# A small fetch of q ahead of lam, fillers regrouped, and three pieces of work moved between engines, in a linear-attention kernel with an MLP

## The chip, the cores and the metric

The kernel runs on one core of a Trainium2 chip. The metric is the device time of one execution in microseconds (us), given as the median of several runs. A profile is one more execution of the same program, recorded by the hardware. The core has five engines that run side by side, each through its own list of instructions in order: PE (TensorE, matmuls and transposes), DVE (VectorE), ACT (ScalarE), POOL (GpSimd) and SP (SyncE, here only for starting DMAs). DMAs are started from SP, ACT or POOL; one that is started from ACT or POOL stands in that engine's list like any other instruction.

## The reference

The first half is causal linear attention with a decay `lam` per head, over B = 4 batches, H = 8 heads, S = 768 positions, D = 64 features; the second is an MLP over the 3072 tokens that come out of it, 512 to 2048 to 512 features.

```python
for b in range(nb):                                  # blocks of positions
    intra = einsum('bhic,bhjc->bhij', qb, kb) * Dmask        # lam ** (i - j) for i >= j, else 0
    intra = einsum('bhij,bhjd->bhid', intra, vb)
    inter = einsum('bhid,bhde->bhie', qb * lam_pow, kv_state)
    out[:, :, sl] = intra + inter
    kv_state = lam_block * kv_state + einsum('bhsd,bhse->bhde', kb * rev_pow, vb)
x = out.transpose(0, 2, 1, 3).reshape(B * S, H * D)
h = x @ w_in
result = (h / (1 + exp(-1.702 * h))) @ w_out
```

## The kernel before, in words

**Tiling.** The positions are cut into windows of 128 (`NW` = 6). The first two windows, w = 0 and w = 1 (`w < ND`), are special: each holds 256 positions of two batches, worked as two halves c = 0 and c = 1 (one batch each), with pairs of neighbouring positions folded into one row. The four later windows hold 128 positions of all four batches. Each window gives 512 tokens, and each goes through the MLP as soon as its attention is done.

**What a half of a window goes through.** `load_one` (L84) fetches k, q and v. For c = 0 of window 0, k and q and v come in two DMAs each, heads 0 to 3 and heads 4 to 7 ("groups" g = 0 and g = 1). `do_cast` (L202) multiplies k or q by powers of lam and turns it to bf16; an argument says on which engine, and g picks one group. `turn_pe` (L239) transposes the result on PE with an identity, and a copy (L219 on DVE or L222 on ACT) brings it from PSUM to SBUF as `kT` or `qT`. `cast_v` (L216 on POOL, L222 on ACT) turns v to bf16, in two copies for the first two windows. `d_scores` (L260) multiplies kT by qT, `d_masks` (L271) masks the scores into `sm`, `d_out` (L320) multiplies by v, `d_one` and `d_state` (L283) form the state, `d_inter` (L302) adds its part, and `d_x` copies the sum into `xT`, the input of the MLP.

**Powers of lam.** `lam` is fetched as one row (L105, a DMA started from ACT), spread over 128 partitions by a small fp32 matmul (`lam_p`, L151), and turned on ACT into ln(lam) (L153) and into powers (`kd_pow` and `qd_pow`, L156). ACT loads a function table ahead of that (L110) and another one behind it (L663). The first cast, of k, reads `kd_pow`.

**Fillers.** `fill(n)` (L147) issues n matmuls over a tile of zeros; no one reads their result. They stand in PE's list between the real work of the first 10 us.

**The order.** Everything behind L656 is in an order written out by hand: each engine executes its own instructions in the order of the program, and an instruction waits for the data it reads. For the opening this is: powers; cast and transpose k and then q of half c = 0; POOL waits for q's second group (`gate_pool`, L651, a copy of one element), then starts the DMA of the first piece of `w_in` and of v of c = 1; scores and masks of c = 0; then half c = 1, whose k is cast by POOL (g = 0) and by DVE (g = 1); then `w_in`'s other four pieces and `w_out` are fetched from POOL's list. `end(0, 1)` finishes window 0.

**The MLP.** Window 0 multiplies by `w_in` directly (`mlp1_half` L418, `mlp1` L406, one block `fc` of 128 features at a time) and for `w_out` uses a scheme with seven products in place of eight (`product`, L468), which needs sums of the halves of the weights (`weight_sums`, L432) and of the activations (`g_sums`, L445), formed by DVE. Later windows do the same for `w_in` (`in_product`, L559), with sums of its blocks that `in_sums(g)` forms once (L535) for each of four groups g of blocks. The steps of a window are a string: "I1" is `in_sums(1)`, "gl3" is one `g_sums`, "W01234" is one `weight_sums`, "u" is the end of one product. `GROUPS` (L515) names the blocks of each group: group 0 is blocks 4, 13, 14, 15; group 2 is blocks 5 to 8. Group 0 is the first that window 1's products use. `w_in` lies in five tiles of 2, 3, 4, 4 and 3 blocks; where the blocks of a pair lie in different tiles, as in group 0, `in_sums` issues eight subtractions in place of four.

**Window 1.** Its loads are started by SP behind a gate (L654) that waits for a piece of `w_out`. Its half c = 1 has k and q cast by POOL and both copies of v by ACT; `end(1, 0)`, `scores(1, 1)` and `end(1, 1)` finish its halves, with window 0's last products and window 1's first blocks of the MLP between them.

Of the kernel before, what the change touches and what calls it, by code (L numbers as in the profile page):

```python
# [25 lines left out]
def kernel(  # L26
# [13 lines left out]
    nc = tc.nc  # L40
    f32 = mybir.dt.float32
    bf16 = mybir.dt.bfloat16
    B, H, S, D = q.shape
    P = 128
# [20 lines left out]
    const = ctx.enter_context(tc.tile_pool(name="const", bufs=1))  # L65
# [36 lines left out]
                    load_one(w, c, nm, src[nm])  # L102

    lam_r = const.tile([1, H], f32)
    nc.scalar.dma_start(out=lam_r, in_=bass.AP(tensor=lam.tensor, offset=lam.offset, ap=[[0, 1], [1, H]]))  # L105
    ones = const.tile([1, P], f32)
    nc.vector.memset(ones, 1.0)
# [35 lines left out]
    def fill(n, new=None):  # L143
        if new:
            fill_ps[0] = acc("ps_fill", shape=[P, W], tag=new)
        for _ in range(n):
            nc.tensor.matmul(fill_ps[0], zero[:, 0:P], zero, start=True, stop=True)  # L147

    fill(4, "mm")
    lam_p = ps.tile([P, H], f32, tag="a", bufs=5, name="lam_p")  # L150
    nc.tensor.matmul(lam_p, ones, lam_r, start=True, stop=True)  # L151
    ln_lam = const.tile([P, H], f32)
# [40 lines left out]
    def do_cast(w, c, nm, eng, g=None):  # L193
        if g in (None, 0):
            cast[w, c, nm] = work.tile([P, NP, 2, P] if w < ND else [P, 2, HD], bf16, tag=f"{nm}s{c}",
                                       bufs={"k": 2, "q": 1}[nm], name=f"{nm}s")
        f, x = loaded[w, c, nm], cast[w, c, nm]
        if w < ND:
            pw = {"k": kd_pow, "q": qd_pow}[nm]
            for R in (0, 1) if g is None else (g,):  # L200
                h = slice(4 * R, 4 * R + 4)
                eng.tensor_tensor(x[:, 2 * R : 2 * R + 2].rearrange("p i a (j d) -> p j (i a) d", j=2),  # L202
                                  f[:, h].rearrange("p (j i) (a d) -> p j (i a) d", j=2, a=2),
                                  pw[:, h].rearrange("p (j i) a -> p j (i a)", j=2).unsqueeze(3).to_broadcast([P, 2, 4, D]),
                                  op=MUL)
        else:
            pw = {"k": k_pow, "q": q_pow}[nm]
            n = 2 * H // 4
            for j in range(2):
                eng.tensor_tensor(x.rearrange("p b (r i j d) -> p j (b r) i d", i=2, j=2, d=D)[:, j],  # L210
                                  f.rearrange("p h (a d) -> p (h a) d", a=2).rearrange("p (n j i) d -> p j n i d", j=2, i=2)[:, j],
                                  pw.rearrange("p b (r j i) -> p j (b r) i", i=2, j=2)[:, j].unsqueeze(3).to_broadcast([P, n, 2, D]),
                                  op=MUL)
# [436 lines left out]
    def gate_pool(x):  # L650
        nc.gpsimd.tensor_copy(behind_q, x)  # L651
# [4 lines left out]
    with tc.manual_schedule():  # L656
        for x, i in ((k_pow, i_k), (q_pow, i_q)):
            nc.scalar.activation(x, ln_lam.unsqueeze(1).to_broadcast([P, 2, H]), EXP, scale=i)
        mk_pow(inv_pow, -1.0 * P)
        for j, rows in enumerate((A, Z)):  # L660
            nc.scalar.activation(blk_pow[rows].rearrange("p (r i) -> p r i", i=2),
                                 ln_lam[rows].rearrange("p (r j i) -> p r j i", i=2, j=2)[:, :, j, :], EXP, scale=1.0 * P)
        nc.scalar.activation(warm, q_pow[:, 0, 0:1], GELU)  # L663
        fill(3)
        for nm, copies in (("k", (dve_copy, act_copy)), ("q", (act_copy, dve_copy))):
            for g in range(2):
                do_cast(0, 0, nm, nc.vector, g)
            for g in range(2):
                turn_pe(0, 0, nm, copies[g], g)
                fill(2 - g if nm == "k" else 1 - g)  # L670
        gate_pool(loaded[0, 0, "q"][0:1, H // 2, 0:1])
        load_w_in(0)
        load_one(0, 1, "v", v)
        cast_v(0, 0, (act_copy, act_copy))
        for pp in range(2):
            d_scores(0, 0, pp)
            d_masks(0, 0, pp)
        fill(3)
        do_cast(0, 1, "k", nc.gpsimd, 0)
        for j in range(1, len(IN_CH)):  # L680
            load_w_in(j)
        d_one(0, 0, "mm")
        d_keep(0, 0)
        turn_pe(0, 1, "k", act_copy, 0)
        oa, oz = d_out(0, 0, ("mm", "mm"))
        nc.scalar.copy(seen, oz[:, 3, P - 1 : P])
        do_cast(0, 1, "q", nc.vector, 0)
        do_cast(0, 1, "k", nc.vector, 1)
        do_cast(0, 1, "q", nc.vector, 1)
        turn_pe(0, 1, "q", act_copy, 0)  # L690
        d_inter(0, 0, oz, 0, False)
        turn_pe(0, 1, "k", act_copy, 1)
        d_state(0, 0, states[0, 0], Z)
        turn_pe(0, 1, "q", dve_copy, 1)
        d_x(0, 0, 0, oa, act_copy)
        d_x(0, 0, 1, oz, act_copy)
        cast_v(0, 1, (act_copy, pool_copy))
        for j in range(NCH):
            load_w_out(j)
        for pp in range(2):  # L700
            d_scores(0, 1, pp)
            d_masks(0, 1, pp)
        nc.gpsimd.affine_select(mask, mask, pattern=[[0, 1], [1, P]], channel_multiplier=-1, base=0,
                                compare_op=mybir.AluOpType.is_ge, fill=0.0)
        gate_sync(w_out_sb[1][0:1, 0, 0:2])
        load(1)
        mlp1_half(0, 0, 0)
        d_one(0, 1)
        d_keep(0, 1)
        act_copy(kv_sb[0][:, 0], states[0, 0])  # L710

        def scores(w, c):
            for pp in range(2):
                d_scores(w, c, pp)
            for pp in range(2):
                d_masks(w, c, pp)

        def end(w, c):
            oa, oz = d_out(w, c)
            t = acc("ps_kv", shape=[P, NP, D]) if w else states[w, c]  # L720
            if w == 0:
                nc.scalar.copy(seen, oz[:, 3, P - 1 : P])
            d_state(w, c, t, Z)
            if w == 0:
                d_inter(w, c, oz, 0, False)
            if w and c == 0:
                d_one(w, 1)
            d_x(w, c, 0, oa, act_copy)
            d_x(w, c, 1, oz, act_copy if w and c else dve_copy)
            if w:  # L730
                nc.vector.tensor_tensor(kv_sb[0][:, 2 * w + c], kept[w, c], t, op=ADD)
            else:
                nc.scalar.copy(kv_sb[0][:, 2 * w + c], t)
            if w and c == 0:
                d_keep(w, 1)

        def steps(w, names):
            for s in names.split():
                one_step(w, s)

        end(0, 1)
        for c, fc in ((0, 2), (1, 0), (1, 2)):
            mlp1_half(0, c, fc)
        for fc in range(4, FFC):
            mlp1(0, fc)
            steps(0, {5: "I1", 7: "I3", 9: "I0 gl3 gl1", 11: "W01234 gl2", 13: "W11234 gl4"}.get(fc, ""))
        steps(0, "p1a gh3 gh1 p2a W23124 p1b p2b gh2 gh4 p7l p4l W33124 p1h p2h p7h")
        do_cast(1, 0, "k", nc.vector)
        do_cast(1, 0, "q", nc.vector)
        steps(0, "p6l")  # L750
        turn_pe(1, 0, "k", act_copy)
        steps(0, "p6h")
        turn_pe(1, 0, "q", act_copy)
        steps(0, "p4h o")
        load(2, "kq")
        cast_v(1, 0, (pool_copy, act_copy))
        do_cast(1, 1, "k", nc.gpsimd)
        steps(0, "P50")
        scores(1, 0)
        d_one(1, 0)  # L760
        d_keep(1, 0)
        steps(0, "P51")
        d_even(1, 0, "mm")
        turn_pe(1, 1, "k", act_copy)
        cast_v(1, 1, (act_copy, act_copy))
        do_cast(1, 1, "q", nc.gpsimd)
        steps(0, "P30")
        end(1, 0)
        steps(0, "u I2")
        turn_pe(1, 1, "q", act_copy)  # L770
        steps(0, "P31")
        halves = [(c, fc) for c in range(HF) for fc in HALVES]
        for i, (c, fc) in enumerate(halves):
            if i == 1:
                scores(1, 1)
                d_even(1, 1)
            if i == 3:
                end(1, 1)
            if i == 4:
                x_sums(1)  # L780
            mlp1_half(1, c, fc)
            if i in (1, 2, 3, 4):
                nm = "kq"[(i - 1) % 2]
                do_cast(2, (i - 1) // 2, nm, nc.gpsimd)
                turn_dma(2, (i - 1) // 2, nm)
            if i == 6:
                load(2, "v")
        steps(1, STEPS[1])
        for w in range(ND, NW):
            steps(w, STEPS[w])  # L790
# [30 lines left out]
```

## Time and profile before

| | |
|---|---|
| median of 3 runs | 191.92 us (191.89 to 194.59) |
| the profiled execution's own time | 192.3 us |
| its span, first to last instruction | 190.6 us |
| PE busy | 184.3 us, 2296 matmuls |
| DVE busy | 152.0 us |
| ACT busy | 129.8 us |
| POOL busy | 50.7 us |

A row of the timeline gives the start and the duration in us, the engine, the line of the kernel, the operation, what is written and read, and in brackets how long the engine stood idle ahead of it and what ended that. "PEld" is the load of weights into PE, which may overlap its matmuls; "ACTq", "SPq" and "POOLq" are the issuing sequencers of those engines. The chain of work that ended last is followed back from the last instruction of the program: at each step it goes to what released the instruction, or to the one before it on its engine, so what stands in the chain set the end. The profiled execution is one execution; durations are taken from it, and a difference worked out from them is set against the median of the runs.

### The profile page before, as it was taken

How to read it: one execution, taken by the hardware profiler on the slowest of the kernel's cores; microseconds unless marked ns; L12 is line 12 of the kernel's file. 1: busy time of each engine (PE TensorE's matmuls, PEld its weight loads, DVE VectorE, ACT ScalarE, POOL GpSimd, SP SyncE). 2: the span in 40 equal slices, each digit the busy share in tenths (PEclk: the TensorE clock that was granted, in tenths of full speed). 3: DMA queues.
4: the chain of work that ended last, by engine and by line, in shares of the span. 5: the costliest groups of instructions: out<-in, count | busy, mean ns of one | idle time of the engine just before them, and what ended most of it. 6: DMA issues, size and time to landing. Idle time of an engine off the chain costs nothing.

```text
span 190.6 us, 5527 instructions
## 1 busy us (share of the span) xinstructions
PE 184.3 (97%) x2296; PEld 152.2 (80%) x2296; DVE 152.0 (80%) x282; ACT 129.8 (68%) x242; POOL 50.7 (27%) x69
## 2 busy tenths in 40 slices
PE   7998999999999999999999999999999999999993
PEld 2556646887888888888888888888888888888882
DVE  1787599987856799879799879799789797888950
ACT  4957665169776986388895388885488876597611
POOL 5588000063458000294000393000492000000000
PEclk9999999999999999999999999999999999999999
DMA  5999999996997899988998565999555903300113
GB/s 144 317 292 204 205 206 224 310 302 158 215 276 165 193 221 237 215 192 143 213 236 204 183 164 118 212 242 217 184 142 123 209 1 111 112 5 0 55 56 112
DMA packets 89599, 33.91 MB, mean 178 GB/s; under 512 B 67430, under 2 KB 89446, under 8 KB 89574
## 3 DMA queue, kind: packets, MB, share of 16 engines
q1 hardware_dynamic: 84676, 28.84, 60.5%
q0 software_dynamic: 4896, 4.72, 14.4%
q8 instruction: 18, 0.29, 0.7%
q14 instruction: 7, 0.06, 0.1%
q10 hardware_dynamic: 2, 0.00, 0.0%
HBM read 27.26 MB, written 6.29 MB: 176 GB/s over the span
## 4 chain that ended last, share of the span: by engine, by line
PE 92%; DVE 4%; ACT 2%; issue 0%; ACTq 0%; DVEq 0%
PE ps_X L468 22%; PE ps_hX L559 17%; PE ps_V L468 10%; PE ps_hV L559 8%; PE ps_Q L468 6%; PE ps_h L406 5%; PE ps_h L418 5%; PE ps_hQ L559 4%; DVE sm L271 3%; PE ps_t L239 2%; PE ps_s L339 2%; PE ps_o L394 2%; PE ps_fill L147 2%; PE ps_o L381 1%; PE ps_Z L468 1%; PE ps_s L260 1%
## 5 line engine op out<-in xcount | busy, mean ns | idle before, releaser
L468 PEld LDWEIGHTS <-g_s 128*128 128x128 bf16 x384 | 37.0, 98 | 4.9
L578 ACT ACTIVATE g_sb<-h_sb 128x512 bf16<-128x512 f32 x54 | 32.6, 631 | 1.2 <-DVE h_sb L567 1.2
L559 PEld LDWEIGHTS <-w_in_t 128*128 128x128 bf16 x288 | 28.1, 98 | 3.3
L468 PEld LDWEIGHTS <-g_sb 128*128 128x128 bf16 x288 | 27.5, 98 | 4.1
L222 ACT COPY part<-ps_hX 128x512 f32<-128x512 f32 x32 | 18.3, 587 | 11.5 <-PE ps_hX L559 11.5
L468 PE MATMUL ps_X<-w_out_t,g_s 128*128 128x256 bf16 x192 | 23.3, 273 | 0.0
L559 PEld LDWEIGHTS <-w_in 128*128 128x128 bf16 x216 | 21.1, 98 | 2.5
L559 PE MATMUL ps_hX<-x_s,w_in_t 128*128 128x256 bf16 x144 | 21.6, 272 | 0.0
L445 DVE TENSOR_TENSOR g_s<-g_sb 128x1024 bf16<-128x1024 bf16 x24 | 16.3, 687 | 5.8 <-ACT g_sb L578 5.6
L210 POOL TENSOR_TENSOR ks<-kf,k_pow 128x512 bf16<-128x512 f32 x16 | 16.3, 1042 | 4.8 <-DMA kf<-in_k_dram 4.8
L210 POOL TENSOR_TENSOR qs<-qf,q_pow 128x512 bf16<-128x512 f32 x16 | 16.5, 1056 | 3.1 <-DMA qf<-in_q_dram 3.1
L219 DVE COPY part<-ps_hV 128x512 f32<-128x512 f32 x18 | 12.4, 688 | 5.9 <-PE ps_hV L559 5.9
L651 POOL CAST behind_q<-x_s 1x1 f32<-1x1 bf16 x3 | 0.5, 176 | 58.5 <-DVE x_s L544 58.5
L484 ACT COPY part<-ps_X 128x512 f32<-128x512 f32 (+1 forms) x13 | 6.7, 518 | 13.2 <-PE ps_X L468 13.2
L567 DVE TENSOR_TENSOR h_sb<-part,ps_hX 128x512 f32<-128x512 f32 x18 | 12.3, 681 | 2.6 <-PE ps_hX L559 2.1
L567 DVE TENSOR_TENSOR h_sb<-part,ps_hV 128x512 f32<-128x512 f32 x18 | 12.3, 684 | 1.0 <-PE ps_hV L559 1.0
L468 PE MATMUL ps_X<-w_out,g_sb 128*128 128x256 bf16 x96 | 12.6, 273 | 0.0
L468 PE MATMUL ps_Q<-w_out,g_sb 128*128 128x256 bf16 x96 | 12.5, 273 | 0.0
L567 DVE TENSOR_TENSOR h_sb<-part,ps_hQ 128x512 f32<-128x512 f32 x18 | 12.2, 680 | 0.0
L222 ACT CAST v_sb<-vf 128x1024 bf16<-128x1024 f32 (+1 forms) x14 | 12.0, 869 | 0.0
L578 ACT ACTIVATE g_sb<-ps_hX 128x512 bf16<-128x512 f32 x18 | 10.6, 589 | 1.8 <-PE ps_hX L559 1.8
L468 PE MATMUL ps_V<-w_out_t,g_s 128*128 128x256 bf16 x96 | 11.6, 273 | 0.0
(113 smaller groups left out, 354.3 us busy)
## 6 DMA issues: line engine op xcount, KB each, us to landing
kf<-in_k_dram SPq DMA_DIRECT2D x10, 512.0 KB, 6.4
qf<-in_q_dram SPq DMA_DIRECT2D x10, 512.0 KB, 7.2
vf<-in_v_dram SPq DMA_DIRECT2D x10, 512.0 KB, 6.2
out_dram<-o_sb SPq DMA_DIRECT2D x24, 128.0 KB, 2.4
out_dram<-o_sb SPq DMA_DIRECT2D x12, 256.0 KB, 2.8
w_out<-in_moe_w_out_dram POOLq DMA_DIRECT2D x4, 512.0 KB, 14.2
kf<-in_k_dram SPq DMA_DIRECT2D x4, 256.0 KB, 3.1
qf<-in_q_dram SPq DMA_DIRECT2D x4, 256.0 KB, 4.6
```

Source lines behind the costliest of these rows:

```text
L210: eng.tensor_tensor(x.rearrange("p b (r i j d) -> p j (b r) i d", i=2, j=2, d=D)[:, j], f.rearrange("p h (a d) -> p (h a) d", a=2).rearran ...
L219: nc.vector.tensor_copy(out, in_)
L222: nc.scalar.copy(out, in_)
L271: nc.vector.tensor_tensor(sm.rearrange("p i a s -> p i (a s)"), flat, mask_d.rearrange("p o a b s -> p o (a b s)").to_broadcast([P, 2, 2 * ...
L406: nc.tensor.matmul(h, w_in_sb[j][:, kc, i * P : (i + 1) * P], xT[w][:, kc, :], start=(kc == 0), stop=(kc == KC - 1))
L418: nc.tensor.matmul(h[:, u, :], w_in_sb[j][:, kc, i * P : (i + 1) * P], xT[w][:, kc, cols], start=(kc == 0), stop=(kc == KC - 1))
L445: nc.vector.tensor_tensor(o, x, y, op=f)
L468: nc.tensor.matmul(bank[:, t], x[:, m, t * P : (t + 1) * P], y, start=((n in (1, 2, 7) or own) and t == ts[0] * last and m == 0), stop=(m ...
L484: nc.scalar.copy(part[w, n, t.start][:, t], bank[:, t])
L559: nc.tensor.matmul(bank[:, u], z[:, kc], y[:, kc], start=(n in (1, 2, 7) and u + kc == 0), stop=(kc == 1), skip_group_check=True)
L567: nc.vector.tensor_tensor(h, h_part[w, g, {2: 1, 5: 7, 4: 6}[n]], bank, op=ADD)
L578: nc.scalar.activation(g_of[w][:, a : b + 1 : b - a, 256 * i : 256 * i + 256], bank, GELU)
```

## The change

It has five pieces. (1) A DMA of 128 pieces of 4 bytes out of q's first batch, one to each partition, into a tile that nothing reads, is issued from ACT ahead of the DMA of lam. (2) Of the four fillers ahead of `lam_p` two stay; three behind it become four; the ones behind k's two transposes go from 2 and 1 to 1 and 2, the one behind q's first transpose goes. That makes nine where there were eleven. (3) Group 1 of k of half c = 1 of window 0 is cast by POOL right behind group 0, ahead of the DMAs of the other four pieces of `w_in`; DVE loses it. (4) The sums of group 2 of `w_in` are formed beside those of group 1, and the sums of group 0 take the place that group 2's had, behind "u". (5) In window 1 the second copy of v of half c = 1 goes from ACT to POOL, behind POOL's cast of q.

```diff
     lam_r = const.tile([1, H], f32)
+    first_q = const.tile([P, 1], f32)
+    nc.scalar.dma_start(out=first_q, in_=bass.AP(tensor=q.tensor, offset=q.offset, ap=[[H * S * D // P, P], [1, 1]]))
     nc.scalar.dma_start(out=lam_r, in_=bass.AP(tensor=lam.tensor, offset=lam.offset, ap=[[0, 1], [1, H]]))
...
-    fill(4, "mm")
+    fill(2, "mm")
     lam_p = ps.tile([P, H], f32, tag="a", bufs=5, name="lam_p")
...
-        fill(3)
+        fill(4)
         for nm, copies in (("k", (dve_copy, act_copy)), ("q", (act_copy, dve_copy))):
             for g in range(2):
                 do_cast(0, 0, nm, nc.vector, g)
             for g in range(2):
                 turn_pe(0, 0, nm, copies[g], g)
-                fill(2 - g if nm == "k" else 1 - g)
+                fill(1 + g if nm == "k" else 0)
...
         do_cast(0, 1, "k", nc.gpsimd, 0)
+        do_cast(0, 1, "k", nc.gpsimd, 1)
         for j in range(1, len(IN_CH)):
             load_w_in(j)
...
         do_cast(0, 1, "q", nc.vector, 0)
-        do_cast(0, 1, "k", nc.vector, 1)
         do_cast(0, 1, "q", nc.vector, 1)
...
-            steps(0, {5: "I1", 7: "I3", 9: "I0 gl3 gl1", 11: "W01234 gl2", 13: "W11234 gl4"}.get(fc, ""))
+            steps(0, {5: "I1 I2", 7: "I3", 9: "gl3 gl1", 11: "W01234 gl2", 13: "W11234 gl4"}.get(fc, ""))
...
         turn_pe(1, 1, "k", act_copy)
-        cast_v(1, 1, (act_copy, act_copy))
         do_cast(1, 1, "q", nc.gpsimd)
+        cast_v(1, 1, (act_copy, pool_copy))
         steps(0, "P30")
         end(1, 0)
-        steps(0, "u I2")
+        steps(0, "u I0")
```

## The prediction

> **What bounds the kernel now.** I read the busy shares first, then the waits of PE behind the opening, then the chain of the first 60 us.
>
> ```profile
> PE 184.3 (97%) x2296; PEld 152.2 (80%) x2296; DVE 152.0 (80%) x282; ACT 129.8 (68%) x242; POOL 50.7 (27%) x69
> ...
> PE ps_kv L283 <- ACT v_sb L222: 0.3, 1, 0.3
> ```
>
> PE is busy nearly throughout, and the second row is all that PE's matmuls waited for from 18.2 us to the end: 0.3 us for the copy of v. So what the opening (up to 18.1) gains or loses reaches the end, and little else can. The chain of the opening:
>
> ```profile
> 1.39 1.89 PE ps_fill L147 x4
> ...
> 3.84 0.19 ACT ln_lam L153
> ...
> 4.64 0.70 DVE ks L202
> ...
> 8.17 0.59 ACT qT L222
> ...
> 8.80 0.47 PE ps_s L260 x16
> ...
> 9.33 2.48 DVE sm L271 x4
> ...
> 12.47 0.40 PE ps_t L239 x4
> ...
> 13.84 0.34 PE ps_t L239 x4
> ...
> 14.63 2.42 DVE sm L271 x4
> ```
>
> Four fillers, (lam's matmul,) ACT's logarithm and powers, the cast of k, (transposes with fillers between them,) the copy of qT, scores, DVE's masks, PE's transposes of c = 1, masks again: a serial chain. Whatever brings 8.80 forward brings 14.63 forward.
>
> **Pieces 1 and 2: lam, the fillers and q.** Is lam late today, or are the fillers? The DMA view of 1.66 to 1.70 us, then the timeline:
>
> ```profile
> q10 hardware_dynamic: 2, 0.00, 2.5%
> ...
> 0.81 0.51 ACTq L105 DMA_DIRECT2D lam_r<-in_lam_dram  x1
> 1.34 1.28 ACT L110 ACT_TABLE_LOAD   x1 [1.34 <-PEq L805]
> 3.21 0.50 PEld L151 LDWEIGHTS lam_p<-lam_r,ones 1*128 1x128 f32 x2 [0.83 <-issue]
> ```
>
> ACT's queue moved two packets in the whole program, lam and its signal, both by 1.70 us, 0.87 after the issue began. lam's weights are loaded at 3.21, just as the four fillers end (1.39 + 1.89 = 3.28): the fillers hold lam back by 1.5 us. One filler lasts 0.63 with its tail (the row at 7.07 further down), so four in 1.89 follow each other by (1.89 - 0.63) / 3 = 0.42; with two fewer, lam's matmul can start 0.85 earlier, near 2.36.
>
> The added fetch takes one slot of ACT's sequencer, as long as lam's 0.51, so lam is issued near 1.34 and its packets move near 2.21. I add nothing more for eight 4-byte packets on each of 16 engines. This is the unknown: below, no wait at all (lam's 0.87 is whole); above, lam stands behind a fetch that is as slow as k's first group, which took the minimum here:
>
> ```profile
> DMA to landing us min/median/max: 2.9/3.1/5.0
> ...
> 9.51 1.06 POOL L202 TENSOR_TENSOR ks<-kf,kd_pow 128x512 bf16<-128x512 f32 x1
> ...
> 6.38 1.28 DVE L202 TENSOR_TENSOR qs<-qf,qd_pow 128x512 bf16<-128x512 f32 x2
> 6.98 0.72 POOL L651 COPY behind_q<-qf 1x1 f32<-1x1 f32 x1 [3.59 <-DMA qf<-in_q_dram]
> DMA to landing us min/median/max: 4.5/4.6/4.8
> ```
>
> 0.81 plus 2.9 is 3.7. I take the row that is nearest in size, lam's own. ACT's table load moves too, from 1.34 to about 1.87, and ends at 3.15; ln(lam) then starts near 3.17 in place of 3.84. So the cast of k starts up to 0.67 earlier, at 3.97, which k's landing (0.81 + 2.9 = 3.71 for the first group) allows, with 0.26 to spare for the packets that the fetch puts between k's on the same DMA engines.
>
> From there q decides. Its two groups are issued at about 1.86 and 2.4, so by the last row above they land at 6.4 and 6.9, and POOL's copy, released by the landing, starts at 6.98. DVE casts q from 6.38 and 6.98: both casts start as the data lands. Two casts take 1.28 and start 0.60 apart, so one takes 0.68, and the first ends at 7.06. Today its transpose waits behind a filler until 7.50:
>
> ```profile
> 7.50 0.63 PE L239 MATMUL ps_t<-ident,qs 128*128 128x128 bf16 x4
> 7.32 0.59 ACT L222 COPY kT<-ps_t 128x512 bf16<-128x512 bf16 x1
> ```
>
> After the change PE works ahead: four fillers end near 4.7 as the first cast of k does, transpose 0.42, filler 0.42, transpose 0.42, two fillers 0.85: free near 6.9. The transpose of q starts at 7.1 in place of 7.50, and ACT, whose list is 0.67 earlier, has its copy of kT done by 7.24 (today 7.91). qT's copy starts 0.40 earlier. **Term: -0.40**, and no more, if q lands as today.
>
> Can q land earlier? The windows view of the opening, whose last two columns are the DMA share and GB/s:
>
> ```profile
> 1.40:2.40 1.00, 1.00 (x3) 0.42 (x4) 0.00 (x0) 1.00 (x1) 1.00 (x4) 1.00 0.18 38
> 4.00:5.20 1.20, 1.19 (x3) 0.15 (x1) 0.56 (x1) 1.10 (x7) 0.00 (x0) 1.00 0.82 200
> 5.60:6.80 1.20, 1.20 (x8) 0.65 (x7) 1.10 (x3) 1.18 (x2) 0.00 (x0) 1.00 1.08 322
> ```
>
> q's 512 KB stand in the queue behind k's 512 KB, which have landed by 1.34 + 3.1 = 4.4; so the rate of 200 GB/s from 4.0 to 5.2 is q's, and 322 is its end and v's start. Against 322 it loses 1.2 x (1 - 200/322) = 0.45 us. If touching q early removes that, q lands 0.45 earlier and the fillers (6.9) bind, with lam: -0.65 in place of -0.40. No row shows a touched tensor, so it is a rival.
>
> **Piece 3: k of c = 1 on POOL.** POOL takes 1.06 for one group (the row at 9.51), so the second ends near 11.63; its transpose comes behind the one of 12.47 (12.07 after the gain) in PE's order. DVE loses one cast of 0.6, but between the two chain rows at 12.47 and 13.84 stand only PE's transposes, `d_inter` and `d_state`, without a gap; PE, not DVE, sets 13.84, so nothing is won there: 0. Behind it on POOL stand four DMAs of `w_in`, the cast of v and `w_out`, all 1.06 later:
>
> ```profile
> 10.50 3.03 POOL L181 DMA_DIRECT2D w_in<-in_moe_w_in_dram  x4
> 14.48 0.61 POOL L216 CAST v_sb<-vf 128x512 bf16<-128x512 f32 x1 [0.95 <-DMA vf<-in_v_dram]
> ...
> w_in<-in_moe_w_in_dram POOLq DMA_DIRECT2D x2, 384.0 KB, 8.8
> ...
> 22.04 0.43 DVE L535 TENSOR_TENSOR w_in_t<-w_in 128x512 bf16<-128x512 bf16 x1 [1.67 <-DMA w_in<-in_moe_w_in_dram]
> 23.96 0.29 DVE L535 TENSOR_TENSOR w_in_t<-w_in,w_in 128x256 bf16<-128x256 bf16 x1 [0.36 <-DMA w_in<-in_moe_w_in_dram]
> ...
> 25.63 0.28 DVE L535 TENSOR_TENSOR w_in_t<-w_in,w_in_t 128x256 bf16<-128x256 bf16 x1
> ```
>
> POOL waited 0.95 for v of c = 1, which stands ahead of them on the same queue until 14.4; a later issue at 11.6 still finds that queue full. So they should land as now: cost 0, with 0.95 of the 1.06 hidden by POOL's own wait. Without that cover: the last piece landed at 23.96 after an issue near 12.8, 11.2; two such pieces average 8.8, so the first of them took 6.4 and landed near 16.9. PE needs it at 18.1 (the start of the long run of window 0's blocks), 17.6 after the gain; 1.06 later it costs 0.35. DVE's waits at 22.04 and 23.96 are off the chain.
>
> A rival price is the shared path of POOL and DVE. These rows:
>
> ```profile
> 54.92 1.16 DVE L544 TENSOR_TENSOR x_s<-xT,x_s 128x512 bf16<-128x512 bf16 x1
> 54.70 2.28 POOL L210 TENSOR_TENSOR qs<-qf,q_pow 128x512 bf16<-128x512 f32 x2 [3.07 <-DMA qf<-in_q_dram]
> ```
>
> A subtraction of that shape takes 0.42 alone (the row at 47.71 below); beside a POOL cast it took 1.16. POOL's added cast (10.57 to 11.63) lies mostly beside masks, which take 2.48 for four with a POOL cast beside them (from 9.51) and 2.42 later; only its last 0.2 to 0.3 meets the cast of q, then at about 11.4, and that is the end of this cost: 0 to 0.3, taken 0. The Trainium skill, GPSIMD Engine Reference, section 8 (Key points), says that GpSimd contends with DVE instructions that have two SBUF inputs; by that rule the cast of q is exposed and the masks, which read PSUM, are not, and the sum would be 0.3 worse. The pair at 54.70 agrees.
>
> **Pieces 4 and 5: sums and v.** The chain and timelines near 46 and 52 us:
>
> ```profile
> 51.83 0.70 PE ps_o L320 x32
> ...
> 46.59 0.41 PE L283 MATMUL ps_kv<-v_sb,ks 64*64 64x64 bf16 x14 [0.28 <-ACT v_sb L222]
> 42.72 2.04 POOL L202 TENSOR_TENSOR qs<-qf,qd_pow 128x512 bf16<-128x512 f32 x2
> 47.71 0.42 DVE L535 TENSOR_TENSOR w_in_t<-w_in 128x512 bf16<-128x512 bf16 x1
> 49.69 2.48 DVE L271 TENSOR_TENSOR sm<-ps_s,mask_d 128x512 bf16<-128x512 f32 x4 [0.43 <-PE ps_s L260]
> ```
>
> With POOL taking one copy (44.8 to 45.4, behind its cast; the next POOL cast is at 49.58), ACT is done with v some 0.5 earlier and PE's wait of 0.28 goes. But group 0's sums, eight from 23.96 to 25.91 = 1.95, now stand where group 2's four took 1.55 (47.71 to 49.26, 0.43 ahead of 49.69): DVE comes free 0.4 later, at 49.66. Two operations of DVE overlap by about 0.1 (a pair of casts takes 1.28, one 0.68), so the masks can start at 49.58 in place of 49.69: 0.11 of the 0.28 is kept, since PE's `ps_o` (from 51.83, 0.70 long) needs the last mask at 49.69 + 2.48 = 52.17. What is late next is DVE. **Term: -0.11**, bounds -0.28 and 0. Group 2's sums fill DVE's 1.67 of waiting ahead of 22.04: 0 in the opening.
>
> **Sum:** -0.40 - 0.11 = -0.5. The profiled execution's own time is 192.3 (span 190.6), 0.2% over the median; 191.8 there, and 191.92 - 0.5 = **191.4** for the median.
>
> **The rivals.**
>
> *q lands earlier.* The dip is q's first touch, and the fetch takes it out. For: it starts with q and ends before v. Against: v, untouched too, shows none. (If the fetch doesn't do this, the forecast stands: it doesn't count on it.) -0.65 - 0.11 = -0.8: 191.1.
>
> *lam becomes late, and the kernel slower.* Place: lam's row behind 128 packets on ACT's queue. Price: landing at 3.7 in place of 2.2, lam's matmul at 3.75 against 3.21, a loss of 0.54, which the fillers pass on to the copy of qT: +0.54 - 0.11 = +0.43: 192.35. It decides from the point where lam lands behind 3.2, 1.0 later than I reckon. For: the first DMA of k starts slowly as well (38 GB/s before 2.4 us). Against: lam's own 0.87.
>
> *Matmuls stay slow longer.* A filler of 512 columns, before and behind 7.9 us:
>
> ```profile
> 7.07 0.63 PE L147 MATMUL ps_fill<-zero 128*128 128x512 bf16 x1
> 7.92 0.44 PE L147 MATMUL ps_fill<-zero 128*128 128x512 bf16 x1
> ```
>
> It takes 0.63, then 0.44: PE's pace rises near 7.9, though the granted clock reads 1.00 all along (the column ahead of the DMA share above). Two fillers fewer, and PE idle until lam, could delay that. Price: the chain's PE pieces behind 7.9, first `ps_s` 0.47, then 1.7 from 12.47 to 14.18 (13.84 + 0.34); twice as long, +0.5 to +2.2; the first is nearer, as the change keeps PE fuller from 3 to 7 us: 191.9, at worst 193.6. The Trainium skill, TensorE: Matmul & The Clock Gate, Part 1, ties the pace to a free-running window of activity of about 3.4 us, and Part 4 says that transposes don't count as activity; by these, fewer fillers could cost a window, and the sum would be near 191.9.
>
> *It cancels:* POOL's contention 0.3 and `w_in` 0.35 eat the gain: 191.9 to 192.1.
>
> **How the numbers follow.** Forecast 0.45 (its own range 191.2 to 191.6), q earlier 0.22, lam late 0.14, slow pace 0.09, cancelled 0.10. The range runs from 190.8 (-0.65, -0.28, with 0.2 for the runs' spread) to 192.5 (lam late, and 0.15 for the runs' spread). A measurement here tells about 2% (3.8 us) from no change; only the worst of the slow pace, or an unforeseen wait, comes near: slower 0.03, faster 0.01, within 0.96.
>
> **What would show it.** Right: lam's weights loaded near 2.4, ln(lam) near 3.2, q's casts still at 6.4 and 7.0, the first scores at 8.4, window 0's first L406 block 0.4 earlier, and no PE wait at 46. Wrong: lam's packets behind 3.2 us; a filler over 0.6 us behind 8; q's casts before 6.2 (then more is won); masks of window 1 late behind L535.

## The result, and the profile after

The changed kernel takes 194.01 us in the median, the kernel before, measured beside it, 192.74: a ratio of 1.0056 with a 95% interval of 1.0039 to 1.0072, so 0.8 to 1.4 us slower. Every ratio here is formed over the runs in the faster of two states that the executions fall into, so it isn't the quotient of the medians beside it. On the scale of the prediction (191.92) that is 193.0; forecast were 191.4, and a range up to 192.5. The size is below what counts as slower (2%), but the sign is plain, and it is the wrong one.

The page of the changed kernel, with the busy times, the queues (packets, MB, share of 16 DMA engines) and the chain that ended last:

```profile
PE 184.9 (96%) x2294; PEld 152.6 (80%) x2294; DVE 150.8 (79%) x281; ACT 129.1 (67%) x241; POOL 51.7 (27%) x71
...
q1 hardware_dynamic: 84676, 28.84, 68.8%
...
q10 hardware_dynamic: 146, 0.00, 0.0%
...
PE 76%; DMA 12%; POOL 5%; issue 2%; DVE 2%; ACT 1%; SPq 1%; ACTq 0%; POOLq 0%
```

The kernel before (its q10 has 2 packets, as the prediction shows):

```profile
q1 hardware_dynamic: 84676, 28.84, 60.5%
...
PE 92%; DVE 4%; ACT 2%; issue 0%; ACTq 0%; DVEq 0%
```

Two things stand out. q10, ACT's queue, has 146 packets in place of 2, as the fetch says. But q1, SP's queue, which the change doesn't touch, moves the same 84676 packets and the same 28.84 MB in 14% more DMA time: 0.605 x 190.6 x 16 = 1845 us before, 0.688 x 191.8 x 16 = 2111 us after, 21.8 and 24.9 ns per packet. And DMA and POOL, absent from the chain before, hold 17% of it now.

The opening in the timeline of the changed kernel (start and duration in us; lines are two or three further down than before):

```profile
0.80 0.43 ACTq L106 DMA_DIRECT2D first_q<-in_q_dram  x1
1.26 0.54 ACTq L107 DMA_DIRECT2D lam_r<-in_lam_dram  x1
1.39 2.31 PE L149 MATMUL ps_fill<-zero 128*128 128x512 bf16 x5 [1.39 <-DVE zero L119]
3.92 0.59 PE L153 MATMUL lam_p<-lam_r,ones 1*128 1x8 f32 x2 [0.22 <-DMA lam_r<-in_lam_dram]
4.55 0.18 ACT L155 ACTIVATE ln_lam<-lam_p 128x8 f32<-128x8 f32 x1 [1.44 <-PE lam_p L153]
5.36 1.29 DVE L204 TENSOR_TENSOR ks<-kf,kd_pow 128x512 bf16<-128x512 f32 x2 [4.02 <-ACT kd_pow L158]
7.21 0.59 POOL L653 COPY behind_q<-qf 1x1 f32<-1x1 f32 x1 [3.84 <-DMA qf<-in_q_dram]
9.52 1.07 PE L262 MATMUL ps_s<-qT,kT 64*64 64x128 bf16 x32 [0.25 <-ACT qT L224]
10.52 1.46 PE L149 MATMUL ps_fill<-zero 128*128 128x512 bf16 x3
18.95 2.85 PE L420 MATMUL ps_h<-xT,w_in 128*128 128x256 bf16 x24
```

lam's matmul waits for lam's landing until 3.92; before it started at 3.21. The cast of k is 0.72 later than at 4.64, the scores 0.72 later than at 8.80. The DMA view of the changed kernel from 1.6 to 3.1 us, and from 3.1 to 3.2:

```profile
q10 hardware_dynamic: 144, 0.00, 4.9%
...
q10 hardware_dynamic: 2, 0.00, 1.1%
```

The fetch is 144 packets (128 and 16 signals), and lam's two come behind them, past 3.1 in place of 1.70. Two rows of the kernel before, for what follows:

```profile
18.05 2.84 PE L418 MATMUL ps_h<-xT,w_in 128*128 128x256 bf16 x24
...
49.23 0.64 PE L260 MATMUL ps_s<-qT,kT 64*64 64x128 bf16 x32
```

The opening ends 0.90 later (18.95 against 18.05). Window 1 in the changed kernel, first its timeline:

```profile
42.92 2.04 POOL L204 TENSOR_TENSOR ks<-kf,kd_pow 128x512 bf16<-128x512 f32 x2 [1.21 <-DMA kf<-in_k_dram]
44.93 2.04 POOL L204 TENSOR_TENSOR qs<-qf,qd_pow 128x512 bf16<-128x512 f32 x2
46.91 0.60 POOL L218 CAST v_sb<-vf 128x512 bf16<-128x512 f32 x1
47.57 0.41 PE L285 MATMUL ps_kv<-v_sb,ks 64*64 64x64 bf16 x14 [0.30 <-POOL v_sb L218]
50.21 0.64 PE L262 MATMUL ps_s<-qT,kT 64*64 64x128 bf16 x32
```

and all that PE's matmuls waited for from 18 us to the end (us in total, times, longest):

```profile
PE ps_kv L285 <- POOL v_sb L218: 0.3, 1, 0.3
PE ps_o L322 <- DVE sm L273: 0.2, 1, 0.2
PE ps_s L341 <- DMA qT<-qs: 0.2, 1, 0.2
```

POOL's cast of q starts at 44.93 in place of 42.72, since the loads of window 1 start later (SP's gate opens at 30.54 in place of 29.05) and take longer to land; so the copy of v behind it, which piece 5 gave to POOL, ends at 47.5, and PE waits for it where it was to wait no more. The last row, a transpose by DMA that PE waits for, is new.

### The profile page after: what moved, and what is told of

The parts are those of the page before. It is cut to its first block, busy times and chain, and to the rows that moved or that the text cites. A ratio compares the mean times of both kernels' runs of the same rounds, so it can differ in the third digit from the quotient of the medians.

```text
span 191.8 us, 5524 instructions
## 1 busy us (share of the span) xinstructions
PE 184.9 (96%) x2294; PEld 152.6 (80%) x2294; DVE 150.8 (79%) x281; ACT 129.1 (67%) x241; POOL 51.7 (27%) x71
## 3 DMA queue, kind: packets, MB, share of 16 engines
q1 hardware_dynamic: 84676, 28.84, 68.8%
q0 software_dynamic: 4896, 4.72, 14.6%
## 4 chain that ended last, share of the span: by engine, by line
PE 76%; DMA 12%; POOL 5%; issue 2%; DVE 2%; ACT 1%; SPq 1%; ACTq 0%; POOLq 0%
PE ps_X L470 18%; PE ps_hX L561 15%; PE ps_V L470 9%; PE ps_hV L561 7%; PE ps_h L408 5%; PE ps_Q L470 5%; DMA vf<-in_v_dram 4%; DMA qf<-in_q_dram 4%; PE ps_hQ L561 4%; PE ps_s L341 2%; PE ps_o L396 2%; DMA qT<-qs 2%; POOL qs L212 2%; PE ps_t L241 1%; PE ps_h L420 1%
## 5 line engine op out<-in xcount | busy, mean ns | idle before, releaser
L224 ACT CAST v_sb<-vf 128x1024 bf16<-128x1024 f32 (+1 forms) x13 | 11.4, 887 | 1.1 <-DMA vf<-in_v_dram 1.1
```

The costliest lines, as they stand in the source:

```text
L224: nc.scalar.copy(out, in_)
```

## The experiments

All kernels compute the whole of the reference; the fetch and the padding are read by nothing. Ratios are to the kernel before, on the same chip (its median was 192.63, 192.50 and 192.63 us in the three groups).

### Which piece? The fetch

My first theory was the one that the opening suggests: the fetch makes lam late, and the rest is as forecast. The rival: the loss comes from the other pieces (fillers, POOL, sums). The first run takes the fetch out of the change, the second puts the fetch alone into the kernel before:

```diff
 # no_fetch: the changed kernel without
-    first_q = const.tile([P, 1], f32)
-    nc.scalar.dma_start(out=first_q, in_=bass.AP(tensor=q.tensor, ...))
 # fetch_only: the kernel before with these two lines
```

> All of the change but the fetch of q. Theory A (the fetch makes lam late: lam's matmul waits for its landing until 3.92 us in the changed kernel, 0.7 behind the kernel before): lam's weights are loaded before 2.8 us, ln(lam) starts by 3.3 and the cast of k by 4.1; the first scores come at 8.4 to 8.8, and the time is 1.0 to 1.6 us under the changed kernel, at or a little under the kernel before (ratio to before 0.997 to 1.001). Theory B (the fewer fillers keep PE slow: fillers behind the first scores take 0.42 each until 11.9 us): the fillers at about 10 us still follow each other by 0.42 and the time stays over the kernel before by 0.1 to 0.3%. Theory C (POOL's added cast delays w_out and window 1's loads): window 1's first POOL cast of k still starts 1.5 us or more later than 40.7, and the time stays 0.1 to 0.2% over.

> The kernel before with the fetch alone. Theory A: lam's matmul moves from 3.2 to about 3.9 us, the cast of k from 4.64 to about 5.35, the long run of window 0's blocks from 18.1 to 18.8; the time is 0.6 to 0.8 us over the kernel before (ratio 1.003 to 1.004). Theory B: nothing of the slow pace, as all fillers stand: the fillers behind the first scores take 0.82 for three as before. Theory C: the fetch costs nothing that lasts: ratio 0.999 to 1.001. If the fetch also brings q in earlier, q's casts start no later than k's copy allows and the loss is under 0.7.

Without the fetch: 192.57 us, ratio 1.0012 (0.9985 to 1.0039), q1 at 60.9%. The fetch alone: 194.07, ratio 1.0072 (1.0051 to 1.0094), q1 at 68.8%. The second is more than any of the theories had (1.004 at most). The whole loss belongs to the fetch, with all that it brings along, and the other four pieces together bring nothing that is measured. Then: is it that lam is late?

```diff
 # fetch_behind: the changed kernel with the two DMAs in the other order
     nc.scalar.dma_start(out=lam_r, ...)
+    first_q = const.tile([P, 1], f32)
+    nc.scalar.dma_start(out=first_q, ...)
 # fillers_only: the kernel before with piece 2
-    fill(4, "mm")
+    fill(2, "mm")
...
-        fill(3)
+        fill(4)
...
-                fill(2 - g if nm == "k" else 1 - g)
+                fill(1 + g if nm == "k" else 0)
```

> The whole change, with the fetch issued behind lam in place of ahead of it. Theory A: lam's packets move at 1.7 us as in the kernel before, its matmul starts before 2.8; the time is the one of the change without the fetch, within 0.2 us, or up to 0.3 under it if touching q early brings q's first group in before 6.2 us. If the touch does nothing for q, q's casts start at 6.4 and 7.0 as before. Theory B: as without the fetch, PE's slow pace lasts past 10 us, 0.1 to 0.3% over the kernel before.

> The kernel before with the fillers of the change alone. Theory A: lam's weights are loaded before 2.8 us, k's cast by 4.1, scores 0.3 to 0.4 earlier than 8.80; ratio to before 0.997 to 0.999. Theory B: PE's pace rises later than 8 us (a filler over 0.6 behind 8 us), the scores take 1.0 in place of 0.7, and the gain of 0.4 is lost: ratio 1.000 to 1.003. The kernel with the whole change but the fetch differs from this one only by the pieces on POOL, DVE and ACT: theory C says that this one is faster by 0.2 to 0.4 us.

With the fetch behind lam, lam's matmul is back at 3.21, and the kernel still takes 193.68 us, 1.0047 (1.0024 to 1.0070), with q1 at 68.4%. **So the first theory fell:** lam's lateness isn't the main part. The fillers alone: 192.64, 1.0012 (0.9987 to 1.0037), nothing; the timeline of this kernel says why they can't gain:

```profile
1.39 1.89 PE L147 MATMUL ps_fill<-zero 128*128 128x512 bf16 x4 [1.39 <-DVE zero L117]
3.20 0.59 PE L151 MATMUL lam_p<-lam_r,ones 1*128 1x8 f32 x2
3.73 1.03 PE L147 MATMUL ps_fill<-zero 128*128 128x512 bf16 x2
```

Four fillers stand ahead of lam's matmul, two behind it, though the program issues two and four. The opening up to L656, with lam's matmul in it, isn't in the order written out by hand. By the order in which PE ran them, the planner, which orders that part, let two of the four behind go ahead; in the changed kernel three (five ahead, in the row at 1.39).

### Why the fetch? The tile, not the transfer

What does a fetch of 128 words do to SP's queue for 190 us? Two theories were left. S: the 4-byte tile takes 32 bytes of each partition, and every tile allocated behind it moves by 32 bytes. In the compiled program the tiles of the loads (from `kf` on) and of the casts and transposes began at multiples of 256 bytes (the first at 96512 = 377 x 256), and now begin 32 bytes behind one. H: it is the use of ACT's queue on all 16 DMA engines that slows SP's.

```diff
 # shift_only: the kernel before with a tile of the same size, no fetch
+    spare = const.tile([P, 1], f32)
+    nc.vector.memset(spare, 0.0)
 # after_padded: the changed kernel, the fetch into the first word of 256 bytes
-    first_q = const.tile([P, 1], f32)
+    first_q_tile = const.tile([P, 64], f32)
+    first_q = first_q_tile[:, 0:1]
 # behind_padded: the same, with the fetch behind lam
```

> The kernel before with one unread tile of 4 bytes per partition more, set by one DVE memset, and no fetch: every tile behind it lies 32 bytes further on, so the tiles that the loads and the DMA transposes write no longer start at multiples of 256 bytes (96512 becomes 96544). Theory S (the fetch's tile shifts the others, and DMAs into shifted tiles are slower): SP's queue takes 68 to 69% of the span in place of 60.5%, the transposes land in 3.0 to 3.2 us in place of 2.7, window 1's POOL cast of k starts 1.5 us or more later than 40.7, and the time is 0.3 to 0.6% over the kernel before. Theory H (the fetch put ACT's queue to use on all 16 DMA engines, and that slows SP's queue from then on): 60.5%, 2.7 us, ratio 0.999 to 1.001.

> The whole change, with the fetch's tile 256 bytes per partition wide in place of 4 (4 bytes are fetched as before), so the tiles behind it start at multiples of 256 bytes again. Theory S: SP's queue is back at 60 to 61%, the transposes at 2.7 us, and what is left over the kernel before is the late lam alone: lam's matmul at 3.7 to 3.9 us, 0.5 to 0.9 us in the end (ratio 1.002 to 1.005), 0.3 to 0.7 us under the changed kernel. Theory H: 68 to 69% and the time of the changed kernel, ratio 1.005 to 1.007.

> The whole change, with the fetch behind lam and its tile 256 bytes wide. Theory S: neither loss is left: lam's matmul at 3.2, SP's queue at 60 to 61%, the time that of the change without the fetch or of the kernel before (ratio 0.998 to 1.001); if the touch helps q, q's casts both start by 6.4 and it is the lower end. Theory H: 68 to 69%, ratio 1.004 to 1.006, as with the fetch behind lam and a narrow tile.

The tile without a fetch: 193.66 us, 1.0059 (1.0036 to 1.0083), q1 at 68.2%. The fetch with the tiles where they were: 192.71, 1.0026 (1.0004 to 1.0049), q1 at 60.2%, and behind lam 192.79, 1.0023 (0.9999 to 1.0048), q1 at 59.7%. The last ratio lies above what was expected (0.998 to 1.001), with an interval that just reaches 1; what it is made of is open. **S is shown and H refuted:** the loss of 1.0059 comes with the shift and without a fetch, and q1's share goes with the tile, not with the fetch. The DMA view of 100 to 140 us, deep in the MLP, where nothing of the opening is left, for the kernel before:

```profile
q1 hardware_dynamic: 23469, 7.48, 74.6%
```

for the one with only the shift:

```profile
q1 hardware_dynamic: 25306, 7.94, 91.0%
```

and for the changed kernel with padding:

```profile
q1 hardware_dynamic: 23942, 7.60, 75.8%
```

Worked out (share x 40 us x 16 engines / packets) that is 20.3, 23.0 and 20.3 ns per packet. The loads and the DMA transposes of the kernel with only the shift (count, size, median us from issue to landing; the last two without a size):

```profile
kf<-in_k_dram SPq DMA_DIRECT2D x10, 512.0 KB, 7.6
...
kT<-ks SPq DMA_TRANSPOSE x8, 3.1
qT<-qs SPq DMA_TRANSPOSE x8, 3.3
```

Before:

```profile
kf<-in_k_dram SPq DMA_DIRECT2D x10, 512.0 KB, 6.4
...
kT<-ks SPq DMA_TRANSPOSE x8, 2.7
qT<-qs SPq DMA_TRANSPOSE x8, 2.7
```

The average hides how the packets lengthen. A row of k, q or v is 64 x 4 = 256 bytes in the later windows. Counted in the traces' own packet records, 99.5% of q1's 65536 packets of 256 bytes (the transposes' among them) took 18 ns or less in the kernel before and in both padded ones; with only the shift it is 67.1%, and the others take 28.5 ns on average. So two packets of three cost what they did, and the rest pay 10 ns more.

The Trainium skill, DMA: Bandwidth & Descriptors, section "How a descriptor splits into AXI transactions", says that a descriptor which starts at a multiple of 256 bytes is cut into transactions of 256 bytes and a leftover, and that a transaction must start at such a multiple, so that one which begins elsewhere starts at the multiple below. By that rule a row of 256 bytes that starts 32 bytes behind a multiple takes two transactions in place of one, an estimate. The traces agree that such a start costs time (13% per packet on average), but not that every packet pays, and the page words the rule for what is read, while here the place that is written was shifted. That rows start off a multiple of 256 is shown as the cause; what happens inside the DMA isn't.

The padded kernels keep what the fetch itself does. In the one with the fetch ahead, lam's matmul starts at 3.84 and the opening ends at 18.86, 0.81 later than before; its ratio is some 0.5 us with an interval of 0.1 to 0.9. In the one with the fetch behind, lam is at 3.20, and POOL's copy behind q's landing stands at 7.47 (6.98 before): q didn't land earlier for having been touched. The profiled execution of this one was the longest of its 12 (194.19 us).

### Which tiles, and how far from 256?

```diff
 # shift128: the kernel before
+    spare = const.tile([P, 32], f32)
+    nc.vector.memset(spare, 0.0)
 # loads_shifted: shift_only, and a pool of 224 bytes between the loads' and the casts' tiles
     ld = ctx.enter_context(tc.tile_pool(name="ld", bufs=2))
+    pad = ctx.enter_context(tc.tile_pool(name="pad", bufs=1))
...
+    pad_t = pad.tile([P, 56], f32)
+    nc.vector.memset(pad_t, 0.0)
 # weights_aligned: the kernel before
+    pad_a = const.tile([P, 24], f32)      # ahead of v_sb, w_in, w_out: from 160 behind 256 to 0
...
+    pad_b = const.tile([P, 40], f32)      # behind them: the later tiles at multiples of 256 again
```

> The kernel before, with a tile of 128 bytes per partition that nothing reads, so that every later tile starts 128 bytes further on: the tiles of the loads and of the transposes at 128 behind a multiple of 256. If only a start at a multiple of 256 bytes is cheap: q1's share 67 to 69%, transposes landing in 3.0 to 3.2 us, the time 0.5 to 0.7% over the kernel before, as with 32 bytes. If a start at a multiple of 64 or 128 is enough: share 60 to 61%, 2.7 us, ratio within 0.2% of 1.

> The kernel before with every constant, every weight and the tiles of the loads 32 bytes further on, but the tiles behind them (casts, transposed k and q, activations, outputs) again at multiples of 256: only what the loads and the weights write is shifted. If the loads make the loss: kf's loads land in 7 us or more (6.4 before), the ratio is 1.004 to 1.007, and the transposes stay at 2.7 us. If the transposes, read and written in shifted tiles, make it: loads at 6.4, the ratio within 0.2% of 1. If both take part: share of q1 between 62 and 67%, ratio 1.002 to 1.004.

> The kernel before with two tiles of padding, so that the tiles of w_in and w_out, at 160 behind a multiple of 256 before, also start at multiples of 256; the loads' and the transposes' tiles stay at such multiples. By the theory of the shifted tiles the 4 MB of weights take 13 to 20% less time on the DMA queues: w_in's last pieces land up to 1 us earlier, the gate of window 1 opens 0.5 to 1 us before 29.05, q1's share falls to 59 to 60%. PE waits for none of them, so the time stays: ratio 0.998 to 1.000. If only the loads that turn or widen a row are hurt, nothing changes at all.

A shift of 128 bytes: 193.15 us, 1.0035 (1.0012 to 1.0057), q1 at

```profile
q1 hardware_dynamic: 84676, 28.84, 68.8%
```

so for the queue 128 is as costly as 32 (68.2%). The time is below the 0.5 to 0.7% expected, perhaps a little less than with 32; the intervals overlap. With only the loads (and the weights and constants ahead of them) shifted: 193.48 us, 1.0060 (1.0037 to 1.0083), and on the page's DMA part

```profile
q1 hardware_dynamic: 84676, 28.84, 67.3%
...
kf<-in_k_dram SPq DMA_DIRECT2D x10, 512.0 KB, 7.4
...
kT<-ks SPq DMA_TRANSPOSE x8, 2.7
qT<-qs SPq DMA_TRANSPOSE x8, 2.7
```

The transposes are back at 2.7 us and the whole loss is there: **the loads make it**, and slow transposes aren't needed for it. (The weights are shifted too, but POOL's queue, which fetches them, stays at 14.4%.) The weights at multiples of 256: 192.72 us, 1.0005 (0.9985 to 1.0026). Here my expectation was wrong in its means: POOL's queue, which fetches the weights, has

```profile
q0 software_dynamic: 4896, 4.72, 14.6%
```

where it had 14.4% before. In the profiled execution, one of the longer ones of this kernel (193.75 us), `w_out` even landed late, and the gate of window 1 opened at 31.15 in place of 29.05. POOL's pieces are larger (4.72 MB / 4896 = 964 bytes), so a further transaction would weigh less; that is argued, not shown.

### The fillers that really stand behind

To have two fillers ahead of lam's matmul and no more, the four behind it were given weights that need `lam_p`, a second tile of zeros:

```diff
 # two_fillers: no_fetch with
-    def fill(n, new=None):
+    def fill(n, new=None, weights=None):
...
-            nc.tensor.matmul(fill_ps[0], zero[:, 0:P], zero, start=True, stop=True)
+            nc.tensor.matmul(fill_ps[0], zero[:, 0:P] if weights is None else weights, zero, start=True, stop=True)
...
+    zero2 = const.tile([P, P], bf16)
+    nc.vector.tensor_tensor(zero2.rearrange("p (a b) -> p a b", a=H), zero[:, 0:P].rearrange("p (a b) -> p a b", a=H),
+                            lam_p.unsqueeze(2).to_broadcast([P, H, P // H]), op=MUL)
...
-        fill(4)
+        fill(4, weights=zero2)
 # best: two_fillers without piece 3, with the padding of weights_aligned
```

> The change without the fetch, where the four fillers behind lam's matmul load their weights from a second tile of zeros that DVE writes once lam's matmul is done (one operation of 0.2 to 0.3 us more), so they cannot stand ahead of it and lam's matmul does stand behind two fillers. If the step of the prediction holds: lam's weights are loaded at 2.3 to 2.6 us, ln(lam) starts by 3.2, the cast of k by 4.0, the scores at 8.4 (0.4 earlier than 8.80), and window 0's long run of blocks 0.3 to 0.4 earlier than in the change without the fetch (18.2): ratio to before 0.997 to 1.000. If lam lands later than its packets say: lam's matmul waits to about 3.2 and nothing is won. If PE's pace rises later, as PE idles longer: the scores start at 8.4 but take 1.0, and the gain is lost by the masks.

> A version put together from what held: two fillers ahead of lam's matmul with the others kept behind it, no fetch, k of half c = 1 cast by POOL and DVE as before, the sums and the copy of v as changed, and all tiles of weights at multiples of 256 bytes. The opening's term of -0.4 and the weights' earlier landing give 0.998 (0.996 to 1.000) of the kernel before: long run of blocks from 17.6 to 17.7. If matmuls' pace decides the opening more than lam, 1.000 or above.

The timeline of the first:

```profile
2.35 0.59 PE L151 MATMUL lam_p<-lam_r,ones 1*128 1x8 f32 x2
...
8.45 0.64 PE L263 MATMUL ps_s<-qT,kT 64*64 64x128 bf16 x32 [0.30 <-ACT qT L225]
...
17.66 2.84 PE L421 MATMUL ps_h<-xT,w_in 128*128 128x256 bf16 x24
```

lam at 2.35 and the end of the opening at 17.66, 0.39 earlier than before, are what the prediction worked out (2.36, and -0.40). The time over all runs doesn't show it: 192.73 us, 1.0002 (0.9978 to 1.0027), though the profiled run, with a span of 190.1, was 0.5 shorter than before; it was the fastest of its 12 (191.79 us). The second kernel does: 192.08 us, 0.9969 (0.9951 to 0.9987), 0.25 to 0.94 us faster than the kernel before and the lowest ratio of all. Its opening ends at 17.72 and its span is 190.2, as good as the first one's. What it has over the first is k of c = 1 shared between POOL and DVE as before, and the aligned weights; alone, the latter gave nothing. Whether the former does isn't shown: no run has it alone, and the intervals of the two kernels overlap.

## Why the prediction was wrong

**The step that failed first: what the fetch costs.** "The added fetch takes one slot of ACT's sequencer [...] I add nothing more": the step counted the DMA and not the tile it lands in. The tile has no instruction and no row in a profile of before, but it moved the tiles of all loads of k, q and v off a multiple of 256 bytes. It is worth 1.0059 (0.7 to 1.6 us) alone, as much as the whole 1.0056. No rival had it; I bounded the transfer's cost from both sides and took for granted that memory costs nothing. With it fell the premise that the opening decides and "little else can": with only the shift the opening ends 0.11 later (18.16 against 18.05) and the span grows by 1.3 (191.9 against 190.6).

**How it reaches the end.** By the casts of window 1. The kernel with only the shift, in PE's timeline:

```profile
40.73 0.40 PE L241 MATMUL ps_t<-ident,qs 128*128 128x128 bf16 x4 [0.20 <-DVE qs L204]
...
45.05 0.40 PE L241 MATMUL ps_t<-ident,ks 128*128 128x128 bf16 x4 [0.25 <-POOL ks L204]
...
47.59 0.41 PE L285 MATMUL ps_kv<-v_sb,ks 64*64 64x64 bf16 x14 [0.30 <-ACT v_sb L224]
...
50.22 0.64 PE L262 MATMUL ps_s<-qT,kT 64*64 64x128 bf16 x32
```

The first two waits, for the casts of q of c = 0 and of k of c = 1, aren't there before. PE is 0.11 late at the end of the opening and 0.99 late at the last row (49.23 before). POOL's cast of k starts at 42.95 in place of 40.71: the gate of window 1 opens 1.09 later (30.14), and from there to the cast it takes 1.15 more.

In the changed kernel the last two rows stand at 47.57 and 50.21, though its opening ended 0.8 later. The kernel with only the loads shifted has them at 47.60 and 50.23, and the one with the fetch behind lam the scores at 50.16. So the two losses don't add: with 32 bytes off, PE waits for the casts of window 1, and an opening that is 0.1 or 0.9 late arrives at the same place. (The other two shifted kernels stand to either side: the scores at 50.58 with the fetch alone, at 49.59 with 128 bytes.) In the changed kernel with padding the wall is gone:

```profile
46.71 0.61 PE L286 MATMUL ps_kv<-v_sb,ks 64*64 64x64 bf16 x32
...
49.55 0.64 PE L263 MATMUL ps_s<-qT,kT 64*64 64x128 bf16 x32
```

both without a wait, on an opening as late as 18.86. But the shift isn't the only way to that wall. The kernel with the padding and the fetch behind lam, in its long execution, has the gate at 30.42 and the scores at 50.50, and the one with the weights aligned has the gate at 31.15 and the scores at 50.64, both with q1 near 60%. The gate waits for `w_out` and opens at different times in the profiled executions, from 29.05 to 31.15. So the path above is one that single executions show; that the shift costs time rests on the runs.

**lam late: the wrong end of the bound.** I took lam's own row (landing near 2.21) and not k's (3.7), "the row that is nearest in size". Size was the wrong measure: the fetch is 144 packets, and lam landed past 3.1, PE's matmul waiting until 3.92. The packets' own time isn't it either: 0.049 x 1.5 us x 16 / 144 is 8 ns for one, so nine on an engine take under 0.1 us. What spread them over more than a microsecond isn't shown. Nor does PE start with the packets: lam's two move between 3.15 and 3.20 us in the changed kernel and its weights are loaded at 3.92; with two fillers and no fetch they move between 1.65 and 1.70 and the load, released by the DMA, starts at 2.35. Both times some 0.7 lies between, so even packets near 2.21 would have meant a matmul near 2.9 and not 2.36. The rival "lam becomes late" had a price of 0.54 by the time of lam's matmul; measured were 0.71 there and 0.81 to 0.90 at the opening's end, since the wait was for 3.9 and not 3.75, and matmuls ran slowly for longer. It held 0.14 and should have led. What it costs in time isn't told apart: with the padding the fetch ahead of lam gives 1.0026 and the fetch behind it 1.0023. In the changed kernel's profile the wall hides it.

**Two fillers fewer.** "With two fewer, lam's matmul can start 0.85 earlier" was right as mechanics (2.35 against 2.36) and wrong as a reading of the change: the planner moved fillers ahead of lam's matmul, so the edit didn't do this. That the change doesn't do what it says was a rival I should have priced, as the opening isn't ordered by hand. Where it was made true, the opening's -0.40 came out as -0.39, and PE's `ps_kv` behind window 1's masks, at 52.48 before, stood at 51.97: 0.51 earlier, the prediction's whole sum. That is one execution; the runs (1.0002) don't show it.

**Matmuls slow longer: it happens, cause open.** Fillers behind 8 us take 1.46 for three in the changed kernel (from 10.52), 0.82 before. But fewer fillers don't decide it. Without the fetch:

```profile
8.80 1.07 PE L260 MATMUL ps_s<-qT,kT 64*64 64x128 bf16 x32 [0.23 <-ACT qT L222]
```

and with the fetch behind lam:

```profile
8.80 0.69 PE L262 MATMUL ps_s<-qT,kT 64*64 64x128 bf16 x32 [0.25 <-ACT qT L224]
```

These two have the same list on PE with the same starts up to there (they differ in the fetch and the 32 bytes), and one runs the scores in 1.07 and the other in 0.69. The rule of the Trainium skill that the prediction quotes (TensorE: Matmul & The Clock Gate, Part 1), a window of activity that runs by itself, would allow that, as the same list may fall differently in the window; no run tests it.

**q earlier: refuted.** The DMA rate from 4.0 to 5.2 us was 248 in place of 200 GB/s in the changed kernel, but that was later k (its loads of 256 KB landed in 4.6 us in the median, 3.1 before) ahead of later q; POOL's copy behind q's landing stands between 6.86 and 7.85 in the five kernels with the fetch (7.21 in the changed one, 6.86 with the padding) and between 6.64 and 7.48 in those without (6.98 before; 6.64 with two fillers): a scatter, and no gain of 0.45.

**Piece 3, pieces 4 and 5.** Without the fetch, PE's wait of 0.28 at 46 is gone and a wait of 0.3 for DVE's masks stands in its place,

```profile
PE ps_o L320 <- DVE sm L271: 0.3, 1, 0.3
```

as the prediction had it ("what is late next is DVE"). POOL's later `w_in`, 1.06 us by the sum, made no wait of PE in that kernel: 0, as taken. From the start of the long run of blocks to that `ps_kv` the kernel before takes 34.43 us (18.05 to 52.48) and the one without the fetch 34.31 (18.23 to 52.54): 0.12 less, where the term was 0.11. The runs can't tell that apart. In the changed kernel piece 5 is worth nothing, because POOL's copy stands behind casts that the late loads hold up.

## What to carry to other kernels

A new buffer, however small, is a change to the address of all that is allocated behind it: compare the addresses of what DMAs write before and after, and keep the tiles that rows of 256 or 512 bytes are loaded into at multiples of 256. A transfer of few bytes isn't short for that (here 512 bytes in 128 pieces held lam until past 3.1 us), so what is urgent on the same queue goes ahead of it. And an edit that moves work across a line that a planner orders is to be read from PE's list, not from the program.

## What the hardware showed that I had not expected

A shift of 32 bytes lengthens the mean DMA time of a packet from 20.3 to 23.0 ns and a DMA transpose from 2.7 to 3.1 or 3.3 us, deep in the MLP as well as in the opening. It does so by making one packet of 256 bytes in three slow, not by making each a little slower. By the beats of 32 bytes that the Trainium skill counts (DMA: Bandwidth & Descriptors, section "How a descriptor splits into AXI transactions"), 32 bytes off would cost a row of 256 bytes 9 in place of 8 and 128 bytes off 12, an estimate by its rule. The queue's share was 68.2% and 68.8%, so the measurement speaks against the beats as the price; by the same rule both shifts make two transactions of a row, which would fit, but no run tests the count of transactions by itself.
